# Linear attention, a top-2 mixture of experts and a squared-ReLU MLP on one core: the order of the k'v sums, where rows are normed, and the size of an untaken path

## The chip, the cores and the metric

The kernel runs on one core of one Trainium2 chip. The metric is the device time of one execution in microseconds (us). All times in this text come from the page of one profiled execution, from answers of its trace, or from the list of timed runs.

## The reference

Three layers follow each other on 2304 rows (4 batches of 576) of 512 columns (8 heads of 64):

```python
kv = np.einsum('bhsd,bhse->bhde', k, v)            # 64x64 per batch and head
out = np.einsum('bhsd,bhde->bhse', q, kv)
out = out / sqrt(mean(out * out, -1) + 1e-6) * g_norm
logits = x @ w_gate;  noisy = logits + log1p(exp(x @ w_noise)) * noise
top2, top2_w = two largest of 8 experts, softmax over the two
out[rows of e] += top2_w * (relu(x[rows of e] @ w1[e]) @ w2[e])     # 512 -> 1024 -> 512
h = relu(x @ w_in);  y = (s * h * h + b) @ w_out                     # 512 -> 2048 -> 512
```

## The kernel before

The 2304 rows are 18 tiles of 128 rows: per pair of batches eight tiles of main rows and one tile (8 and 17) of the 64 last rows of both batches.

**The front** (about the first 94 us) makes the normed attention rows. The helper `kv(b, h0, h1)` sums k'v of the heads h0 to h1 into one PSUM tile: for every head four products over 128 rows (the main rows, line 344) and then one over the 64 last rows (line 345). Even heads write partitions 0 to 63 of the tile, odd heads 64 to 127. `warm(n)` issues n products on a constant, whose result nobody reads. A batch's products are asked for in two halves or at once, between tiles, as the table KV_AT says (batch 1 after tile 1, batch 2 after tiles 5 and 6, batch 3 after tiles 10 and 11).

The loop over tiles t is written out by hand, and each engine takes its instructions in that order: transposes of q for tile t+1 (`q_tr`, line 404, evicted by ScalarE in line 406); the copy of q for tile t+3 (`repack`, on DVE up to tile 9, on POOL from tile 10, line 394); the inverse norm of tile t-1 (`inv_rms`, ScalarE lines 443 and 444, POOL lines 446 to 448); the product with k'v (`att`, line 415); its eviction (line 426), squares (430) and sums of squares (DVE, line 434) in `squares`, which also ends the inverse norm of tile t-1 (`inv_end`, DVE line 455, then POOL line 457); the logits of tile t-1 (`norm`, DVE line 465); and the store of a row tile to `xs` in DRAM (`put_rows`, SP line 470). A stored row has 520 columns: 512 unnormed ones and 8 inverse norms. From tile 9 on, the gating of the first nine tiles is spread over these steps by `tick()`: its small DVE and POOL instructions end in a list of rows `idx_e` (line 535) and two gathers from `xs` on POOL's queue (line 187). The rows are multiplied by their inverse norms after the gather (`normed`, line 211, DVE), transposed (line 378), and split into a high and a low part (lines 381 and 382). Then the experts' first product starts (lines 808 to 810). SP's queue carries loads of q, k and v, the stores to `xs`, and from tile 12 on the weights; `advance(n)` splits the weights of unit n-1 (ScalarE lines 146 and 153, DVE 148, POOL 154) and loads two units ahead.

**The main part** runs 16 groups of row blocks. Every step is a first product (`l1`), side work from a table of steps, and a second product (`l2`, lines 832 to 834). Side work brings in the next group's rows: gather, `normed`, transposes, split.

**The general path** `general()` stands after step 20. It handles inputs in which one expert gets more rows than its blocks hold. Two flags are loaded into registers, and each engine jumps over the path's two parts when they are zero, as here. The second part (from line 888) holds eight copies of `block`, one for each expert, and each copy has its eight steps over the hidden columns written out.

Of the kernel before, what the change touches and what calls it, by code (L numbers as in the profile page):

```python
# [8 lines left out]
F32 = mybir.dt.float32  # L9
# [7 lines left out]
OP = mybir.AluOpType  # L17
# [4 lines left out]
def kernel(  # L22
# [62 lines left out]


    XS = DM + H
    NROW = 8
# [119 lines left out]

    def normed(r):
        x = r[:, :DM].rearrange("p (h d) -> p h d", h=H)  # L210
        nc.vector.tensor_mul(x, x, r[:, DM:][:, :, None].to_broadcast([P, H, D]))
        return r[:, :DM]


# [53 lines left out]

    warm(12)

# [66 lines left out]
    def kv(b, h0=0, h1=H):  # L337
        K, V, KR, VR = (KQV[b, n] for n in ("k", "v", "kr", "vr"))
        ps = KVP[b] = KVP.get(b) or small_ps([P, NP, D])
        for h in range(h0, h1):  # L340
            hp, i = divmod(h, 2)
            o = ps[i * D:(i + 1) * D, hp, :]
            for j in range(NJ):
                nc.tensor.matmul(o, lhsT=K[:, h, j, :], rhs=V[:, h, j, :], start=j == 0, stop=False)
            nc.tensor.matmul(o, lhsT=KR[:, h, :], rhs=VR[:, h, :], start=False, stop=True)
        if h1 == H:
            KVP[b] = kvc = pool.tile([P, 2, 2, D], F32, name="kvc", bufs=1)
            nc.scalar.activation(kvc, ps.rearrange("p (s a) d -> p a s d", s=2), AF.Copy)
            for i in range(2):
                r = slice(i * D, (i + 1) * D)  # L350
                nc.scalar.activation(kvbd[b][r, :, i * HW_:i * HW_ + D], ps[r], AF.Copy)
# [86 lines left out]
    def inv_rms(t):  # L438
        raw, ss, x = AT[t]
        y = pool.tile([P, H], F32, name="iv", bufs=3)  # L440
        u = pool.tile([P, H], F32, name="iu", bufs=2)
# [9 lines left out]
    def inv_end(t):  # L451
        if t < 0:
            return
        raw, u, y, x = AT[t]
        nc.vector.scalar_tensor_tensor(x[:, DM:], u, 1.5, y, op0=OP.add, op1=OP.mult)
        yb = x[:, DM:].rearrange("p (a b) -> p a b", a=NP)[:, :, :, None]
        nc.gpsimd.tensor_mul(raw, raw, yb.to_broadcast([P, NP, 2, W2C]))
        AT[t] = (raw, x)

    def norm(t):  # L460
        pl, x = AT.pop(t)
        tick()
        tick()
        tick()
        nc.vector.tensor_reduce(lg[:, t, :], pl.rearrange("p a b c -> p c (a b)"), axis=AX, op=OP.add)
        XO.append((t, x))
# [72 lines left out]
    def gate_rank(g):  # L539
# [12 lines left out]
        if g == 0:  # L552
            yield from early_table(0, NT0, 0, EB, idx_e)
            for i in range(EB):
                ROWS[0, i] = gather_rows(0, i)
            yield 7
            for i in range(EB):
                ROWS[0, i] = normed(ROWS[0, i])
            yield 6
            for i in range(EB):  # L560
                put_x(0, ROWS.pop((0, i)), i)
# [152 lines left out]
    kv(0, 0, H // 2)  # L714
    warm(10)
    kv(0, H // 2, H)
    load_batch(2, "kv")
    warm(4)
    mfold_a(0)
# [15 lines left out]
    for t in range(NT + 1):  # L735
# [21 lines left out]
        if t == NT0:  # L757
            chain[:] = [gating(0), 0]
        if t == 12:
            advance(0)  # L760
        if 13 <= t < 17:
            advance(t - 12)
    put_rows()
# [20 lines left out]
    def combine(g, i, rows):  # L784
        if groups[g][0] == "e":
            return normed(rows)
        t = groups[g][2] + i
# [65 lines left out]
    def general():  # L853
# [8 lines left out]
        def block(e, icol, rows_out):  # L862
            ic = gp.tile([P, 1], I32, name="ic", bufs=1)
            nc.vector.tensor_copy(ic, icol)
            gather(rows, xs[:, :], ic)
            normed(rows)
            pt = psum.tile([P, KC, P], F32, name="ph", bufs=3)
            for c in range(KC):
                nc.tensor.transpose(pt[:, c, :], rows[:, c * P:(c + 1) * P], ident)
            nc.vector.tensor_scalar(xT, pt, gcol, None, op0=OP.mult)  # L870
            y = psum.tile([P, DM], F32, name="ph", bufs=3)
            for f in range(NF1):
                a, b = weight_aps(e * NF1 + f)
                nc.sync.dma_start(r1, a)
                nc.sync.dma_start(r2, b)
                ph = psum.tile([P, P], F32, name="ph", bufs=3)
                for c in range(KC):
                    nc.tensor.matmul(ph, lhsT=r1[:, c, :], rhs=xT[:, c, :], start=c == 0, stop=c == KC - 1)
                nc.scalar.activation(h, ph, AF.Relu)
                nc.tensor.matmul(y, lhsT=h, rhs=r2, start=f == 0, stop=f == NF1 - 1)  # L880
            yr = rows[:, :DM]
            nc.vector.tensor_copy(yr, y)
            nc.sync.dma_start(rows_out, yr)
# [4 lines left out]
        with tc.If(v1 > 0):  # L888
# [5 lines left out]
            nc.vector.tensor_scalar(idx_ov, pt, float(N // 2), None, op0=OP.add)  # L894
            for e in range(E):
                ve = nc.values_load(nblk[0:1, e:e + 1], min_val=0, max_val=NT)
                vb = nc.values_load(ovb[0:1, e:e + 1], min_val=0, max_val=OVB)
                with tc.If(ve > MB):
                    with tc.For_i(MB, ve) as blk:
                        block(e, idx_ov[:, e * NT:(e + 1) * NT][:, bass.ds(blk, 1)],  # L900
                              ys[bass.ds((vb + blk - MB) * P, P), :])

# [85 lines left out]
    at(4, rest_of_first)  # L988
    at(6, lambda: [normed(ROWS[1, i]) for i in range(groups[1][3])])
    at(5, lambda: run(gate_slots(1)))  # L990
# [11 lines left out]
    def put_first():  # L1002
        for i in range(groups[1][3]):
            put_x(1, ROWS.pop((1, i))[:, :DM], i)

# [102 lines left out]
```

## Time and profile before

| | us |
|---|---|
| timed runs | 994.40, 994.58, 996.50; median 994.58 |
| the profiled execution | 996.47 |
| its span, first to last instruction | 994.7 |
| PE busy (matmul) | 960.5, 97% of the span |
| DVE busy | 542.3, 55% |
| ScalarE busy | 398.3, 40% |
| POOL busy | 133.5, 13% |

The page gives busy time for each engine and for 40 equal slices of the span (24.9 us each), the clock that was granted to PE, and the share of time in which the 16 DMA engines moved data. Answers of the trace list instructions in order of time: the start, how long it (or a merged run of it) took, engine and line, what it writes and reads, how many, and in brackets how long the engine had been idle before it and what it had waited for. Matmuls overlap each other, so the pitch from one start to the next is shorter than one matmul. A float32 matmul of the program stands in the trace as two.

### The profile page before, as it was taken

To read this page: it belongs to the slowest core of one execution; us is meant where nothing else is said; L and a number is where in the kernel's file an instruction comes from. 1 tells how busy PE (TensorE), PEld (TensorE's weight loads), DVE (VectorE), ACT (ScalarE), POOL (GpSimd) and SP (SyncE) were. 2 spreads that over 40 slices of the span, in tenths; PEclk is the share of its full clock that TensorE was granted. 3 is DMA by queue.
4 is the path that set the end of the run, shared out by engine and by line. 5 is a ranking of instruction groups with operands and counts; after the bars stand their busy time and mean duration, and the time that the engine had idled before them with its cause. 6 is when DMAs were issued, how large, how long until landed. Compare 5 with 4: busy or idle time off the path is not lost.

```text
span 994.7 us, 13902 instructions
## 1 busy us (share of the span) xinstructions
PE 960.5 (97%) x5282; PEld 828.4 (83%) x5282; DVE 542.3 (55%) x1000; ACT 398.3 (40%) x725; POOL 133.5 (13%) x196
## 2 busy tenths in 40 slices
PE   8996998979999999999999999999999999999998
PEld 5875787979999999999999999888788878887886
DVE  1448887545686877767656465434434343443333
ACT  1666334224555555646444444323222232222222
POOL 3256325101010100000000112100110010000000
PEclk8998999989999999999999999999999999999999
DMA  9965767426457584874635532200120021001001
GB/s 264 273 196 177 216 187 234 160 78 235 135 183 267 157 273 153 279 237 150 234 104 193 189 126 79 74 1 11 32 85 1 22 65 41 1 1 43 1 1 42
DMA packets 111854, 129.30 MB, mean 130 GB/s; under 512 B 14208, under 2 KB 80768, under 8 KB 111776
## 3 DMA queue, kind: packets, MB, share of 16 engines
q1 hardware_dynamic: 104320, 108.10, 33.7%
q0 software_dynamic: 6208, 20.17, 7.0%
q8 instruction: 44, 0.72, 0.3%
q14 instruction: 34, 0.28, 0.1%
q10 hardware_dynamic: 1248, 0.03, 0.1%
HBM read 93.07 MB, written 35.20 MB: 129 GB/s over the span
## 4 chain that ended last, share of the span: by engine, by line
PE 76%; DVE 1%; ACT 1%; issue 0%; ACTq 0%
PE ph L809 13%; PE ph L810 13%; PE y L832 12%; PE ph L808 12%; PE y L834 12%; PE y L833 12%; PE sps L378 2%; DVE r L818 0%; DVE xl L382 0%; ACT hh L820 0%; ACT r L817 0%; DVE r L819 0%; DVE hl L821 0%; DVE rows L841 0%; ACT xh L381 0%
## 5 line engine op out<-in xcount | busy, mean ns | idle before, releaser
L809 PE MATMUL ph<-xl,w1h 128*128 128x320 f32 (+3 forms) x832 | 277.4, 333 | 3.1 <-DVE xl L382 3.1
L808 PE MATMUL ph<-xh,w1h 128*128 128x320 f32 (+3 forms) x832 | 276.8, 333 | 1.3 <-DVE xl L382 0.7
L810 PE MATMUL ph<-xh,w1l 128*128 128x320 f32 (+3 forms) x832 | 276.8, 333 | 0.0
L832 PE MATMUL y<-w2h,hh 128*128 128x512 f32 x608 | 244.4, 402 | 5.7 <-PEq L888 5.0
L834 PE MATMUL y<-w2h,hl 128*128 128x512 f32 x608 | 238.9, 393 | 1.2 <-DVE hl L813 1.2
L833 PE MATMUL y<-w2l,hh 128*128 128x512 f32 x608 | 238.8, 393 | 0.0
L809 PEld LDWEIGHTS ph<-xl,w1h 128*128 128x128 f32 x832 | 157.0, 189 | 18.7 <-DVE xl L382 5.1
L808 PEld LDWEIGHTS ph<-xh,w1h 128*128 128x128 f32 x832 | 157.1, 189 | 16.9 <-ACT xh L381 2.3
L810 PEld LDWEIGHTS ph<-xh,w1l 128*128 128x128 f32 x832 | 157.2, 189 | 9.8
L812 ACT ACTIVATE hh<-ph 128x320 fp32r<-128x320 f32 (+2 forms) x128 | 55.9, 438 | 228.7 <-PE ph L810 228.7
L818 DVE SCALAR_TENSOR_TENSOR r<-ph,r 128x512 f32<-128x512 f32 (+1 forms) x80 | 51.1, 638 | 175.9 <-ACT r L817 175.5
L832 PEld LDWEIGHTS y<-w2h,hh 128*128 128x128 f32 x608 | 115.3, 190 | 27.2 <-issue 5.2
L834 PEld LDWEIGHTS y<-w2h,hl 128*128 128x128 f32 x608 | 114.9, 189 | 27.3 <-DVE hl L813 1.6
L813 DVE SCALAR_TENSOR_TENSOR hl<-ph,hh 128x320 fp32r<-128x320 f32 (+2 forms) x128 | 62.3, 489 | 133.3 <-ACT hh L812 132.3
L833 PEld LDWEIGHTS y<-w2l,hh 128*128 128x128 f32 x608 | 115.3, 190 | 20.8
L817 ACT ACTIVATE r<-ph 128x512 f32<-128x512 f32 (+1 forms) x80 | 44.5, 556 | 187.9 <-PE ph L810 187.9
L820 ACT ACTIVATE hh<-r 128x512 fp32r<-128x512 f32 (+1 forms) x80 | 47.1, 589 | 101.2 <-DVE r L819 101.2
L821 DVE TENSOR_TENSOR hl<-r,hh 128x512 fp32r<-128x512 f32 (+1 forms) x80 | 51.1, 639 | 52.6 <-ACT hh L820 52.6
L187 POOL DMA_INDIRECT rows<-xs,idx x35 | 34.5, 985 | 321.7 <-PE sps L378 195.9
L187 POOL DMA_INDIRECT rows<-ys,slot_i x36 | 34.5, 958 | 268.5 <-DVE rows L790 134.3
L148 DVE SCALAR_TENSOR_TENSOR w1l<-raw,gcol,w1h 128x512 fp32r<-128x512 f32 x64 | 50.6, 792 | 15.9 <-ACT w1h L146 15.6
L153 ACT ACTIVATE w2h<-raw 128x512 fp32r<-128x512 f32 x80 | 49.6, 620 | 1.0 <-DMA raw<-in_moe_w_dram 1.0
(166 smaller groups left out, 875.9 us busy)
## 6 DMA issues: line engine op xcount, KB each, us to landing
raw<-in_moe_w_dram SPq DMA_DIRECT2D x128, 256.0 KB, 3.3
ys<-rows SPq DMA_DIRECT2D x40, 256.0 KB, 3.8
c_raw<-in_moe_w_in_dram SPq DMA_DIRECT2D x16, 512.0 KB, 6.2
c_raw<-in_moe_w_out_dram SPq DMA_DIRECT2D x16, 512.0 KB, 7.9
wd<-c_fl SPq DMA_DIRECT2D x16, 512.0 KB, 4.5
raw<-wd SPq DMA_DIRECT2D x32, 256.0 KB, 2.8
ys<-zero SPq DMA_DIRECT2D x13, 512.0 KB, 5.0
xs<-x SPq DMA_DIRECT2D x18, 260.0 KB, 3.8
```

What stands on the lines that cost most here:

```text
L148: nc.vector.scalar_tensor_tensor(l1.rearrange(fl), r1.rearrange(fl), gcol, h1.bitcast(F32).rearrange(fl), op0=OP.mult, op1=OP.subtract)
L187: nc.gpsimd.indirect_dma_start(out=dst, out_offset=None, in_=src, in_offset=bass.IndirectOffsetOnAxis(ap=icol, axis=0))
L808: nc.tensor.matmul(ps[:, :wd], lhsT=w1h[:, c, :], rhs=xh[:, c, cs], start=c == 0, stop=False)
L809: nc.tensor.matmul(ps[:, :wd], lhsT=w1h[:, c, :], rhs=xl[:, c, cs], start=False, stop=False)
L810: nc.tensor.matmul(ps[:, :wd], lhsT=w1l[:, c, :], rhs=xh[:, c, cs], start=False, stop=c == KC - 1)
L812: nc.scalar.activation(hh[:, cs], ps[:, :wd], AF.Relu)
L813: nc.vector.scalar_tensor_tensor(hl[:, cs], ps[:, :wd], 0.0, hh[:, cs].bitcast(F32), op0=OP.max, op1=OP.subtract)
L818: nc.vector.scalar_tensor_tensor(r[:, :wd], ps[:, :wd], 0.0, r[:, :wd], op0=OP.max, op1=OP.mult)
L821: nc.vector.tensor_sub(hl[:, cs], r[:, :wd], hh[:, cs].bitcast(F32))
L832: nc.tensor.matmul(y, lhsT=hh[:, cs], rhs=w2h, start=f == 0, stop=False)
L833: nc.tensor.matmul(y, lhsT=hh[:, cs], rhs=w2l, start=False, stop=False)
L834: nc.tensor.matmul(y, lhsT=hl[:, cs], rhs=w2h, start=False, stop=f == nf - 1)
```

## The change

It has these parts. `kv` runs over the row chunks on the outside and over the heads inside, so that the products over the 64 last rows stand together at the end, and products into partitions 0 to 63 and 64 to 127 alternate; one start flag per half of the partitions serves all heads. The warm-up products change from 12, 10 and 4 to 14, 4 and none. The norm is multiplied into the row tile in `norm`, before the store; a stored row has 512 columns, and `normed` and its calls are gone. Weights are loaded and split one tile earlier. The general path loops over experts and hidden columns by registers, and sums its second product in SBUF.

```diff
-    XS = DM + H
+    XS = DM
-    warm(12)
+    warm(14)
 def kv(b, h0=0, h1=H):
-        for h in range(h0, h1):
-            hp, i = divmod(h, 2)
-            o = ps[i * D:(i + 1) * D, hp, :]
-            for j in range(NJ):
-                nc.tensor.matmul(o, lhsT=K[:, h, j, :], rhs=V[:, h, j, :], start=j == 0, stop=False)
-            nc.tensor.matmul(o, lhsT=KR[:, h, :], rhs=VR[:, h, :], start=False, stop=True)
+        for j in range(NJ + 1):
+            for h in range(h0, h1):
+                hp, i = divmod(h, 2)
+                lh, rh = (K[:, h, j, :], V[:, h, j, :]) if j < NJ else (KR[:, h, :], VR[:, h, :])
+                nc.tensor.matmul(ps[i * D:(i + 1) * D, hp, :], lhsT=lh, rhs=rh, start=j == 0 and h - h0 < 2,
+                                 stop=j == NJ and h >= h1 - 2, skip_group_check=True)
 def inv_end(t):
-        nc.vector.scalar_tensor_tensor(x[:, DM:], u, 1.5, y, op0=OP.add, op1=OP.mult)
+        nc.vector.scalar_tensor_tensor(y, u, 1.5, y, op0=OP.add, op1=OP.mult)
 def norm(t):
         tick()
         tick()
         tick()
+        xv = x.rearrange("p (h d) -> p h d", h=H)
+        nc.vector.tensor_mul(xv, xv, y[:, :, None].to_broadcast([P, H, D]))
         nc.vector.tensor_reduce(lg[:, t, :], pl.rearrange("p a b c -> p c (a b)"), axis=AX, op=OP.add)
 def gate_rank(g):
-            yield 7
-            for i in range(EB):
-                ROWS[0, i] = normed(ROWS[0, i])
-            yield 6
+            yield 12
     kv(0, 0, H // 2)
-    warm(10)
+    warm(4)
     kv(0, H // 2, H)
     load_batch(2, "kv")
-    warm(4)
...
-        if t == 12:
+        if t == 11:
             advance(0)
-        if 13 <= t < 17:
-            advance(t - 12)
+        if 12 <= t < 16:
+            advance(t - 11)
 def combine(g, i, rows):
         if groups[g][0] == "e":
-            return normed(rows)
+            return rows
 def block(e, icol, rows_out):
-            normed(rows)
-            for f in range(NF1):
+            with tc.For_i(0, NF1) as f:
...
-                nc.tensor.matmul(y, lhsT=h, rhs=r2, start=f == 0, stop=f == NF1 - 1)
+                nc.tensor.matmul(y, lhsT=h, rhs=r2, start=True, stop=True)
+                nc.vector.tensor_add(yr, yr, y)
 def general():
-            for e in range(E):
+            with tc.For_i(0, E) as e:
```

Three places show how instructions move. On PE, between tile 1 and tile 2 of the front, the products of batch 1 (`kr` and `vr` are the 64 last rows); a row with x4 stands for four instructions. Before:

```order
L415 MATMUL att<-kvbd_162,qT 128x160 x4
L344 MATMUL sps<-v,k 64x64 x4
L345 MATMUL sps<-vr,kr 64x64
L344 MATMUL sps<-v,k 64x64 x4
L345 MATMUL sps<-vr,kr 64x64
L344 MATMUL sps<-v,k 64x64 x4
```

The pair of rows stands eight times there, once for each head. In the changed kernel:

```order
L410 MATMUL att<-kvbd_164,qT 128x160 x4
L339 MATMUL sps<-v,k 64x64 x32
L339 MATMUL sps<-vr,kr 64x64 x8
L399 MATMUL sps<-ident,qc 128x128 x4
L410 MATMUL att<-kvbd_164,qT 128x160 x4
```

The change from 128-row to 64-row operands is made once and no longer after every head. The second place is DVE, at tiles 12 and 13 of the front, from the tables of the gating (`ohe`) to the list of rows `idx_e`. Before:

```order
L525 TENSOR_SCALAR ohe<-io_188,early 128x256 x9
L465 TENSOR_REDUCE lg<-raw 128x16
L428 COPY raw<-att 128x128
L434 TENSOR_REDUCE ss<-sq 128x8
L455 SCALAR_TENSOR_TENSOR x<-iu,iv 128x8
L465 TENSOR_REDUCE lg<-raw 128x16
L148 SCALAR_TENSOR_TENSOR w1l_81<-raw_970,gcol,w1h_80 128x512
L428 COPY raw<-att 128x128
L535 TENSOR_SCALAR idx_e<-sps 128x2
```

In the changed kernel:

```order
L522 TENSOR_SCALAR ohe<-io_190,early 128x256 x9
L461 TENSOR_TENSOR x<-x,iv 128x512
L462 TENSOR_REDUCE lg<-raw 128x16
L147 SCALAR_TENSOR_TENSOR w1l_81<-raw_896,gcol,w1h_80 128x512
L423 COPY raw<-att 128x128
L429 TENSOR_REDUCE ss<-sq 128x8
L450 SCALAR_TENSOR_TENSOR iv<-iu,iv 128x8
L461 TENSOR_TENSOR x<-x,iv 128x512
L462 TENSOR_REDUCE lg<-raw 128x16
L147 SCALAR_TENSOR_TENSOR w1l_85<-raw_900,gcol,w1h_84 128x512
L423 COPY raw<-att 128x128
L532 TENSOR_SCALAR idx_e<-sps 128x2
```

One 128x512 multiplication (x by iv) per tile has come in, and one more weight split stands ahead of the list. The third place is PE at the general path; shown is the start of the first part's only block. Before:

```order
L885 COMPARE_AND_BRANCH
L886 COMPARE_AND_BRANCH
L886 UNCONDITIONAL_BRANCH x2
L1103 BRANCH_PREFETCH_HINT
L869 MATMUL ph<-ident,xl_2546 128x128 x4
```

After these stand eight times four products (line 878) and one (line 880), 44 products in the block, and the second part has eight such blocks and 36 products on tables. In the changed kernel the whole block is:

```order
L861 MATMUL ph<-ident,xl_2541 128x128 x4
L866 COMPARE_AND_BRANCH
L866 UNCONDITIONAL_BRANCH x2
L1095 BRANCH_PREFETCH_HINT
L872 MATMUL ph<-xh_2540 128x128 x4
L875 MATMUL ph<-gr_2542,xl_2541 128x512
L866 REGISTER_ALU
L866 COMPARE_AND_BRANCH
L866 UNCONDITIONAL_BRANCH
```

Nine products stand in a block instead of 44, and the second part has one block instead of eight beside its 36 products on tables.

## Rows read from the trace of the kernel before

**Rows 1.** The page: PE's busy tenths in 40 equal slices of the span.
```profile
PE   8996998979999999999999999999999999999998
```
**Rows 2.** By stretch: length; busy PE, PEld, DVE, ACT, POOL; PE's clock, DMA share, GB/s.
```profile
50.00:57.00 7.00, 6.09 (x60) 5.12 (x57) 2.14 (x7) 5.33 (x14) 3.42 (x7) 1.00 1.03 312
62.00:70.00 8.00, 8.00 (x87) 6.82 (x86) 5.47 (x17) 4.11 (x10) 4.58 (x13) 1.00 0.19 70
64.10:93.65 29.55, 21.23 (x189) 17.87 (x187) 21.63 (x58) 21.10 (x49) 18.78 (x36) 0.88 0.45 144
220.00:620.00 400.00, 400.00 (x2319) 364.83 (x2318) 263.29 (x409) 202.25 (x346) 37.57 (x40) 1.00 0.56 186
```
**Rows 3.** PE in order of time at k'v of batch 3 and around (start, length, idle).
```profile
53.68 1.31 PE L419 MATMUL att<-kvbd,qT 128*64 128x160 f32 x16
...
57.59 1.99 PE L415 MATMUL att<-kvbd,qT 128*128 128x160 f32 x8 [1.47 <-ACT kvbd L370]
59.37 1.06 PE L404 MATMUL sps<-ident,qc 128*128 128x128 f32 x4
...
62.07 0.68 PE L344 MATMUL sps<-v,k 128*64 128x64 f32 x8
62.68 0.32 PE L345 MATMUL sps<-vr,kr 64*64 64x64 f32 x2
62.93 0.68 PE L344 MATMUL sps<-v,k 128*64 128x64 f32 x8
...
76.29 1.25 PE L415 MATMUL att<-kvbd,qT 128*128 128x160 f32 x8
```
**Rows 4.** SP in order of time: the load of q for batch 3 is issued.
```profile
49.31 0.39 SPq L235 DMA_DIRECT2D q<-in_q_dram  x1
```
**Rows 5.** DMA issues, 40 to 70 us: count, KB, median us from issue to landing.
```profile
q<-in_q_dram SPq DMA_DIRECT2D x1, 1024.0 KB, 7.7
```
**Rows 6.** POOL, then DVE, in order of time at tile 9's inverse norm.
```profile
62.18 1.04 POOL L394 TENSOR_TENSOR qc<-q,ones 128x512 f32<-128x512 f32 x1
...
64.11 0.31 DVE L455 SCALAR_TENSOR_TENSOR x<-iu,iv 128x8 f32<-128x8 f32 x1
```
**Rows 7.** DVE groups from 64.1 to 93.65 us: count, busy us, mean ns, idle before.
```profile
L148 DVE SCALAR_TENSOR_TENSOR w1l<-raw,gcol,w1h 128x512 fp32r<-128x512 f32 x3 | 4.4, 1460 | 0.0
L465 DVE TENSOR_REDUCE lg<-raw 128x16 f32<-128x128 f32 x6 | 2.2, 366 | 3.8 <-POOL raw L457 3.8
L211 DVE TENSOR_TENSOR rows<-rows 128x512 f32<-128x512 f32 x2 | 1.5, 780 | 0.0
```
**Rows 8.** All row multiplications from 80 to 180 us: ns min, median, max.
```profile
L211 DVE TENSOR_TENSOR rows<-rows x10: 677/686/1239, 88.4 to 166.4; 128x512 f32<-128x512 f32 x10
```
**Rows 9.** PE in order of time: the front's end, the first expert group, two later waits.
```profile
82.71 1.35 PE L415 MATMUL att<-kvbd,qT 128*128 128x160 f32 x8 [1.94 <-ACT qT L406]
89.09 1.97 PE L378 MATMUL sps<-ident,rows 128*128 128x128 f32 x8 [5.03 <-DVE rows L211]
...
93.65 0.39 PE L808 MATMUL ph<-xh,w1h 128*128 128x256 f32 x1 [0.74 <-DVE xl L382]
...
163.85 0.93 PE L378 MATMUL sps<-ident,rows 128*128 128x128 f32 x5 [1.27 <-DVE hl L813]
...
173.63 0.41 PE L809 MATMUL ph<-xl,w1h 128*128 128x320 f32 x1 [1.88 <-DVE xl L382]
```
**Rows 10.** PE's sequencer at the general path's two jumps: ns, start.
```profile
L885 PEldq COMPARE_BRANCH  x1: 353/353/353, 208.1 to 208.1; - x1
L888 PEldq COMPARE_BRANCH  x1: 4501/4501/4501, 209.9 to 209.9; - x1
```
**Rows 11.** PE in order of time behind the second jump.
```profile
214.70 0.77 PE L832 MATMUL y<-w2h,hh 128*128 128x512 f32 x1 [5.01 <-PEq L888]
...
218.64 0.39 PE L832 MATMUL y<-w2h,hh 128*128 128x512 f32 x1
218.88 0.40 PE L833 MATMUL y<-w2l,hh 128*128 128x512 f32 x1
```

## What the change was predicted to do

> **What bounds the kernel now.** The first view to read is the page's picture of busy tenths [rows 1]: PE's digits are uneven over the first nine slices, and 9 in nearly every one behind them. The windows confirm it: from 220 to 620 us PE was busy 400.00 of 400.00 us at a granted clock of 1.00, with DVE at 263.29 and ScalarE at 202.25 [rows 2]. So the end is the moment at which that dense stretch starts, plus PE work that the change does not touch. Only what PE loses ahead of about 220 us can be won or made worse: idle time, stretches at the lower clock, and products that take longer than they must. Three places there are touched: the front up to the first expert product at 93.65 us, two waits in the next expert groups [rows 9], and the general path's second jump [rows 10, 11]. The sum is made against the profiled execution (996.47 us); the median of the timed runs, 994.58, lies 1.89 below it, and this is taken off at the end.
>
> **k'v's order.** Before, the next head's products start .86 us behind a head's (62.07 to 62.93) [rows 3]: eight over 128 rows and two over 64 (each float32 product stands twice), so a half call of four heads takes 3.46 us. The eight take .68, and one alone lasts about .22 (an estimate: the .32 of two over 64 rows less a start-to-start of .10), so their pitch is (.68 - .22) / 7 = .065; the last of the eight then starts at 62.53 and the first over 64 rows at 62.68, so a change between 128 and 64 rows costs about .15 in place of a pitch, twice per head. After, a half call has 40 products and one such change: 39 x .065 + .15 = 2.7 us, .75 saved. More is possible where products into the two halves of the partitions run beside each other. The row that shows it is the product with k'v on tile 8, that of the last rows: 16 half-height matmuls in 1.31 us, where eight full ones took 1.25 [rows 3]. With that a half call takes about 1.5 us, 2 saved. Four half calls (batches 1 and 2) stand ahead of batch 3's: 3 to 8 us, if PE is what the front waits for.
>
> **What binds behind it.** It is not PE alone. The load of q for batch 3 was issued at 49.31 and took 7.7 us [rows 4, 5]; it lands at 57.0, with all 16 DMA engines in use from 50 to 57 us (share 1.03) [rows 2], so it comes no earlier. POOL's copy of tile 13 reads that q and stands ahead of tile 9's inverse norm in POOL's queue: it started at 62.18, took 1.04, and DVE ended the inverse norm at 64.11, 1.93 behind its start [rows 6]. With the data at 57.0 that step cannot come before 57.0 + 1.93 = 58.9. This caps PE's gain at 64.11 - 58.9 = 5.2 us, in the middle of the 3 to 8. From here on the front is a race of PE with DVE. In the 29.55 us to the first expert product DVE was busy 21.63 [rows 2]. The change adds six multiplications of 128x512 (one per tile in `norm`, six being the count of L465 there) at .69, the median of the ten [rows 7, 8]: +4.1. It removes the two of `normed`: 2 x .78 = -1.6 [rows 7]. It moves one more weight split ahead of the list `idx_e`: +1.46 [rows 7], or half if it is not slowed. DVE's work becomes 24.9 to 25.6. Of DVE's 7.9 idle us the largest part, 3.8, waits for POOL's product of the logits [rows 7]; the multiplication now lies exactly in that wait, so I keep a third of the idle time, 2.4, as what the added work cannot fill. 58.9 + 25.6 + 2.4 = 86.9, and the first expert product comes at about 87.0 instead of 93.65: **-6.6 us**, with -4 (all idle time stays and splits are slow) to -9 (DVE idles nowhere) as ends.
>
> **What goes with the multiplication.** The 5.03 us for which PE waited on the gathered rows [rows 9] end in DVE's multiplication by the list of waits, but most of it is the gather's own time: behind the gather the rows were multiplied for 2 x .78 us. After, the transposes wait for the gather directly. Since `put_rows` on SP now follows the multiplication, a store starts .69 later than the inverse norm would allow; behind it in SP's queue stand the loads of the weights, at a DMA share of .19 from 62 to 70 us [rows 2], so there is room. The list `idx_e` and the gathers come after all nine early stores in any case. Eight columns fewer in a stored row change nothing that a row here shows.
>
> **Warm-ups.** Two products more at the start, six and four fewer behind k'v's first half and the second. Nearest row of the same width: .24 per product [rows 11], .43 at half clock, so -8 net is 2 to 3.5 us of PE. It is costed at nothing, since the tiles there wait for loads up to the q that lands at 57.0; if that cover were gone it would be a gain of that size. It can also hurt, which is a rival below.
>
> **Expert groups 1 and 2.** The change takes the multiplication out of DVE's queue in the main part, where it stands in front of the evictions that PE waits for. At 163.85 PE waited 1.27 us for hl, at 173.63 1.88 for xl [rows 9], both DVE's. Without 2 x .69 ahead the first goes nearly to zero (-1.1), the second loses .69: **-1.8 us**, between 0 (the rows' arrival is what binds) and -3. Behind 220 us PE has no idle time [rows 2], so some thirty multiplications less on DVE are worth nothing there.
>
> **The general path.** The jump over the first part, one block of 44 products, held PE's sequencer .35 us; the jump over the second, eight such blocks and 36 products on tables, held it 4.50 us [rows 10], and PE was idle 5.01 [rows 11]. Then nine products started .43 us apart (214.70 to 218.64, half clock) instead of .24: 3.94 - 9 x .24 = 1.8 more. After, the second part has 36 products and one block of 9, as long as what the jump of .35 passed. That row is the near one, so I take .3 of stall and no loss of clock: 5.01 - .3 + 1.8 = **-6.5 us**, with 0 as the other end. The Trainium skill ("Runtime: NRT & Kernel Launch", Instruction fetch mechanics) states that a taken branch out of the instructions already fetched waits for a fetch by DMA. The two rows agree in kind, and the same sentence speaks of loops by registers as costly; none of these runs here, so its price would be paid only by the one jump.
>
> **Sum.** 996.47 - 6.6 - 1.8 - 6.5 = 981.57 for a profiled run, less 1.89: **979.7 us**.
>
> **Rivals.** (a) The second jump stalls as before, because what counts is not the length passed but that the target has to be fetched at all. For it: 36 products on tables remain. Against it: the .35 row. No -6.5: 986.2 us. (b) The front gains 1 us instead of 6.6. PE that finishes k'v sooner waits longer for loads, and fewer warm-ups fill that wait; the product and transposes at 57.59 behind an idle 1.47 took 1.99 + 1.06 at half clock, where the same product later took 1.25 [rows 3]. Some seven tiles at 1.99 - 1.25 = .74 more eat 5 of the gain, or DVE's added work does. It gives 985.3 us. The Trainium skill ("TensorE: Matmul & The Clock Gate", Loop structure matters more than you think) warns of just this: matmuls with waits for DMA between them run cold. The 1.99 agrees; by that rule alone the front's part would be near zero and the result that of this rival. (c) Slower: DVE is the front's bound from its first tile, and each of 18 multiplications stands on the path, 18 x .69 - 1.6 = +10.8. With -6.5 and -1.8 that is +2.5: 997.1 us. It decides where DVE has no idle time left; against it, DVE was busy 2.14 of 7.00 us from 50 to 57 [rows 2]. (d) Better: halves run beside each other everywhere, q is copied as soon as it lands, and with waits shorter than about 1.3 us PE keeps its clock: -9.5 in the front, -3 in the groups and -7.5 at the jump: 974.6 us.
>
> **How the numbers follow.** The forecast has .52, (a) .15, (b) .15, (d) .10, (c) .08. The forecast's own ends, with one term off at a time, run from 976 to 983; the range reaches to (a) and (b) above and (d) below: 974 to 987. It leaves out (c) and the outer halves of the others, about .18. About 0.2%, 2 us, is what a measurement of this kernel can tell from no change. Only (c) can lie there or above: .03 within, .05 slower; the other .92 is faster.
>
> **What the changed profile would show.** At the second jump: a sequencer row near .35 instead of 4.50 and full pitch behind it; with a row of 4 us, (a) holds. In the front: k'v's 40 products of a half call in under 2.7 us; POOL's copy of tile 13 near 57; the first expert product near 87; PE's transposes behind the gather waiting for a DMA and not for DVE. If PE's pitch of .43 and clock below 1.00 fill more of the front, (b) holds; if DVE is busy without a break up to the list, (c) does. In the groups: the waits of 1.27 and 1.88 shorter. I would be wrong in kind if the dense stretch at 220 us started earlier by 15 us and the end did not follow, which would mean that something behind it waits for other than PE.

## The result and the profile after

The changed kernel took 983.37 us (median of four runs, 982.76 to 986.96) against 995.54 for the kernel before (four runs, 994.40 to 999.86): a ratio of .9877, interval .9838 to .9916. A second set of five runs gave 983.98 and .9881 (.9863 to .9900). Forecast were 979.7 us and a gain of 14.9 us; the gain is 12.2 in the first set and 10.9 in the second. The profiled execution after has a span of 982.0 us, 12.7 less than before. Sign and range held; two of the three terms of the sum came out smaller than said and one larger, for reasons that the forecast did not have.

The page after: PE's busy tenths and its clock in 40 slices, which answer to [rows 1].

```profile
PE   7866999999999999999999999999999999999998
...
PEclk7987999999999999999999999999999999999999
```

The later slices that read 8 and 7 before are 9 now; the first three are lower than before (786 against 899). PE has less to do there and waits more: 4.0 us in sum for loads of v, and once 5.5 us for DVE. Windows of the changed kernel follow (length; busy PE, PEld, DVE, ACT, POOL; granted clock, DMA share, GB/s), as in [rows 2]:

```profile
59.09:87.83 28.74, 16.61 (x114) 14.62 (x112) 24.55 (x60) 17.19 (x39) 19.94 (x36) 0.73 0.50 163
...
79.00:92.50 13.50, 9.29 (x45) 7.66 (x45) 10.61 (x27) 7.53 (x18) 9.28 (x18) 0.50 0.69 223
106.30:109.70 3.40, 3.40 (x14) 3.03 (x13) 3.40 (x10) 0.00 (x0) 1.32 (x1) 0.50 0.80 232
...
220.00:620.00 400.00, 399.24 (x2312) 363.56 (x2311) 250.42 (x390) 201.94 (x348) 39.76 (x41) 1.00 0.55 184
```

From 220 us on PE is as dense as before (399.24 of 400). DVE has 13 us less work there (250.42 against 263.29 in [rows 2]), and nothing comes of it. So the end still follows the start of the dense stretch.

PE of the changed kernel in order of time (start, length, engine and line, tiles, count, in brackets the idle time before and what it waited for), against [rows 3, 9]:

```profile
52.47 1.15 PE L339 MATMUL sps<-v,k 128*64 128x64 f32 x32
53.55 0.45 PE L339 MATMUL sps<-vr,kr 64*64 64x64 f32 x8
53.93 0.66 PE L399 MATMUL sps<-ident,qc 128*128 128x128 f32 x4
...
66.12 0.50 PE L542 MATMUL sps<-g,onesb 128*128 128x72 bf16 x9 [5.50 <-DVE g L510]
...
83.60 1.97 PE L373 MATMUL sps<-ident,rows 128*128 128x128 f32 x8 [3.63 <-DMA rows<-xs,idx_e]
85.50 2.40 PE L414 MATMUL att<-kvbd,qT 128*64 128x160 f32 x16
87.83 0.58 PE L801 MATMUL ph<-xh,w1h 128*128 128x256 f32 x1
...
92.36 0.41 PE L802 MATMUL ph<-xl,w1h 128*128 128x256 f32 x1
92.57 0.32 PE L803 MATMUL ph<-xh,w1l 128*128 128x256 f32 x1
```

A half call of k'v takes 53.93 - 52.47 = 1.46 us instead of 3.46. PE's lead then turns into a wait of 5.50 us for the gating on DVE. The transposes behind the gather wait for the DMA and no longer for DVE, and the first expert product stands at 87.83. From 79.0 to 92.5 us the clock is .50 of full speed (1.2 of 2.4 GHz), so the expert products start .21 us apart (92.36 to 92.57) until then.

The steps that the forecast took as binding in the front are on SP, POOL and DVE. SP's row comes first (the load of q for batch 3 is issued), then the DMA, POOL (the copy of tile 13), and DVE (the inverse norm of tile 9, then the list of rows):

```profile
47.78 0.41 SPq L229 DMA_DIRECT2D q<-in_q_dram  x1
```

```profile
q<-in_q_dram SPq DMA_DIRECT2D x1, 1024.0 KB, 9.3
```

```profile
57.17 1.04 POOL L389 TENSOR_TENSOR qc<-q,ones 128x512 f32<-128x512 f32 x1 [2.56 <-PE sps L339]
```

```profile
59.09 0.28 DVE L450 SCALAR_TENSOR_TENSOR iv<-iu,iv 128x8 f32<-128x8 f32 x1 [3.28 <-POOL iu L443]
...
77.26 0.14 DVE L532 TENSOR_SCALAR idx_e<-sps 128x2 int32<-128x2 f32 x1
```

The q lands at 47.78 + 9.3 = 57.1, and POOL starts .1 us behind it. The bracket on POOL's row names PE; a wait for several events is put down to one of them, and the landing time tells which it was (in the second profile of this kernel, further down, the copy again starts .1 us behind the landing, and the row names the load). DVE's groups from 59.09 to 87.83 us (count, busy us, mean ns, idle before), as in [rows 7]:

```profile
L147 DVE SCALAR_TENSOR_TENSOR w1l<-raw,gcol,w1h 128x512 fp32r<-128x512 f32 x4 | 5.1, 1276 | 0.0
L461 DVE TENSOR_TENSOR x<-x,iv 128x512 f32<-128x512 f32 x6 | 4.1, 686 | 0.1
...
L462 DVE TENSOR_REDUCE lg<-raw 128x16 f32<-128x128 f32 x6 | 2.2, 364 | 3.3 <-POOL raw L452 3.3
```

And the general path: the sequencer's jump, PE on both sides of it, and DVE, as in [rows 10, 11]:

```profile
L882 PEldq COMPARE_BRANCH  x1: 339/339/339, 202.3 to 202.3; - x1
L882 DVEq COMPARE_BRANCH  x1: 56/56/56, 204.5 to 204.5; - x1
L882 DVEq EVENT_SEMAPHORE  x2: 21/21/21, 207.3 to 207.4; - x2
```

```profile
202.93 0.47 PE L825 MATMUL y<-w2h,hh 128*128 128x512 f32 x1 [0.84 <-PEq L882]
...
207.42 0.39 PE L801 MATMUL ph<-xh,w1h 128*128 128x320 f32 x1 [0.84 <-DVEq L882]
```

```profile
207.56 0.75 DVE L147 SCALAR_TENSOR_TENSOR w1l<-raw,gcol,w1h 128x512 fp32r<-128x512 f32 x1 [4.12 <-DVEq L882]
```

**Where the time went.** Both kernels issue the same 4,320 products of the experts and the last layer, so the nth of one can be laid against the nth of the other; the difference of their starts is what the change has won up to there.

| product | before, us | after, us | difference |
|---|---|---|---|
| first expert product | 93.65 | 87.83 | -5.8 |
| first product of the second kind (`y`) | 97.45 | 93.44 | -4.0 |
| the 91st | 112.17 | 109.26 | -2.9 |
| last before the general path | 208.95 | 201.33 | -7.6 |
| behind it, past DVE's jump | 220.03 | 207.42 | -12.6 |
| the last of all | 989.64 | 976.76 | -12.9 |

So 2.9 us of the front's 5.8 arrive at 112 us, the expert groups up to the general path add 4.7, the general path 5.0, and the rest of the span .3.

### The profile page after: what moved, and what is told of

The parts are those of the page before. It is cut to its first block, busy times and chain, and to the rows that moved or that the text cites. A ratio compares the mean times of both kernels' runs of the same rounds, so it can differ in the third digit from the quotient of the medians.

```text
span 982.0 us, 13843 instructions
## 1 busy us (share of the span) xinstructions
PE 942.6 (96%) x5274; PEld 818.5 (83%) x5275; DVE 529.9 (54%) x979; ACT 397.8 (41%) x726; POOL 140.3 (14%) x197
## 4 chain that ended last, share of the span: by engine, by line
PE 77%; DVE 1%; ACT 1%; issue 0%; ACTq 0%
PE ph L802 13%; PE ph L803 13%; PE ph L801 13%; PE y L825 12%; PE y L826 12%; PE y L827 12%; PE sps L373 2%; DVE r L811 0%; DVE xl L377 0%; ACT hh L813 0%; ACT r L810 0%; DVE r L812 0%; DVE hl L814 0%; DVE rows L834 0%; ACT xh L376 0%
## 5 line engine op out<-in xcount | busy, mean ns | idle before, releaser
L801 PEld LDWEIGHTS ph<-xh,w1h 128*128 128x128 f32 x832 | 158.0, 190 | 17.6 <-ACT xh L376 2.3
L805 ACT ACTIVATE hh<-ph 128x320 fp32r<-128x320 f32 (+2 forms) x128 | 55.9, 437 | 227.0 <-PE ph L803 227.0
L147 DVE SCALAR_TENSOR_TENSOR w1l<-raw,gcol,w1h 128x512 fp32r<-128x512 f32 x64 | 50.7, 793 | 22.3 <-ACT w1h L145 17.6
```

What stands on the lines that cost most here:

```text
L147: nc.vector.scalar_tensor_tensor(l1.rearrange(fl), r1.rearrange(fl), gcol, h1.bitcast(F32).rearrange(fl), op0=OP.mult, op1=OP.subtract)
L801: nc.tensor.matmul(ps[:, :wd], lhsT=w1h[:, c, :], rhs=xh[:, c, cs], start=c == 0, stop=False)
L805: nc.scalar.activation(hh[:, cs], ps[:, :wd], AF.Relu)
```

## The experiments

Medians stand beside the median of the kernel before that was timed along with them. Single runs of the changed kernels spread by some 4 us, so a difference under 2 us is read from the traces or not at all.

**The general path put back.** The edit restores the eight written-out copies of the block:

```diff
-            with tc.For_i(0, E) as e:
+            for e in range(E):
...
-            with tc.For_i(0, NF1) as f:
+            for f in range(NF1):
```

> The changed kernel with the general path as before (eight copies of the block, 44 products each). Theory A, from the two traces laid against each other product by product: the smaller path gives 5.2 us (6.0 on PE, of which .84 is given back in a new wait for DVE behind the jump), so +5.2: 988.6 us, and PE is idle 5 us at the second jump again. Theory B, the forecast's own sum: 6.5, 989.9 us. Theory C: the gain lies elsewhere and a later wait takes it, 983.4 us.

988.57 us (before 995.06; ratio .9940, .9920 to .9959), 5.2 more than the changed kernel's first set of runs and 4.6 more than its second: theory A, while B's 6.5 is not excluded by the intervals. The profiled execution was the slowest of the seven (993.94; its q of batch 3 landed at 59.4), so only the stretch in question is read from it:

```profile
L880 PEldq COMPARE_BRANCH  x1: 3681/3681/3681, 208.0 to 208.0; - x1
```

```profile
211.97 0.77 PE L825 MATMUL y<-w2h,hh 128*128 128x512 f32 x1 [4.19 <-PEq L880]
```

```profile
210.20:217.00 6.80, 5.03 (x12) 3.99 (x13) 1.35 (x2) 1.25 (x2) 0.00 (x0) 0.50 0.32 105
```

The jump stalls again (3.68 us), PE is idle 4.19, and the products behind it run at a granted clock of .50 until 217.0 us. Between the last product ahead of the general path and the one past DVE's jump this kernel gains .3 us on the kernel before, where the changed one gains 5.0.

**The k'v order put back.**

```diff
-        for j in range(NJ + 1):
-            for h in range(h0, h1):
+        for h in range(h0, h1):
+            for j in range(NJ):
```

> The changed kernel with k'v summed head by head as before. Theory A: PE is what the front waits for until the q of batch 3 has landed; POOL's copy of tile 13 starts near 62 instead of 57.2 and the first expert product comes 5 us later, near 93, of which about 3 us reach the end, since a stretch of half clock then lies over other work: 986.4 us. Theory B: loads and DVE bind, PE's order is worth under 1 us: 984 us or less.

991.42 us (before 995.06; .9960, .9946 to .9974): 7.4 to 8.1 more than the changed kernel, above both theories. In its trace the q of batch 3 lands at 55.9, but POOL's copy starts only at 61.35, without an idle time ahead of it, and the first expert product stands at 92.0:

```profile
61.35 1.04 POOL L388 TENSOR_TENSOR qc<-q,ones 128x512 f32<-128x512 f32 x1
```

So it is not the load that the copy follows here, nor PE directly: POOL comes to it from the steps of the tiles before, and these run late. At 52.91 us DVE had waited 2.62 for ScalarE's eviction of a PE product. That is theory A's start near 62, reached by way of DVE and POOL. The profiled execution was the lowest of ten runs (988.30), and its last product comes 4.5 us later than in the changed kernel. What the other runs lost beyond that no trace shows.

**The k'v order alone**, in the kernel before (the same edit the other way round).

> The kernel before with nothing changed but the order of the k'v sums. Theory A: PE was what the front waited for, so POOL's copy of tile 13 starts as soon as its q lands, near 57 instead of 62.2, the multiplication is not yet in DVE's way, and the first expert product comes 5 to 6 us earlier than in the kernel before; with most of it kept to the end: 989.5 to 991 us. Theory B: the order pays only together with the fewer warm-up products, since 14 of them stand in PE's queue ahead of batch 0's second half and behind it; then 992 to 994 us.

989.15 us (before 994.90; .9935, .9918 to .9952): theory A, 5.75 us from this edit with every warm-up product in place. POOL in order of time, then DVE at tile 9's inverse norm:

```profile
59.70 1.04 POOL L395 TENSOR_TENSOR qc<-q,ones 128x512 f32<-128x512 f32 x1 [3.35 <-DMA q<-in_q_dram]
61.62 0.28 DVE L456 SCALAR_TENSOR_TENSOR x<-iu,iv 128x8 f32<-128x8 f32 x1 [3.32 <-POOL iu L449]
```

Now the load is what ends POOL's wait, here at 59.7, since in this run it landed late; the first expert product stands at 88.08 nevertheless. The inverse norm comes only 2.5 us earlier than in the kernel before (61.62 for 64.11), the product 5.6. The rest is won between the inverse norm and the list, which takes 14.5 us (61.62 to 76.14) instead of 17.6 (64.11 to 81.72). DVE's copy out of the product with k'v in that stretch, in the kernel before and here:

```profile
L428 DVE COPY raw<-att 128x128 f32<-128x128 f32 x4 | 1.1, 284 | 2.9 <-ACT x L426 2.9
L429 DVE COPY raw<-att 128x128 f32<-128x128 f32 x4 | 1.1, 275 | 0.0
```

Batch 3's own half calls stood there on PE [rows 3], and DVE waited 2.9 us in all for ScalarE's eviction of products that came late.

**No alternation of the halves.** All even heads, then all odd heads:

```diff
-        for j in range(NJ + 1):
-            for h in range(h0, h1):
+        for j, h in [(j, h) for i in range(2) for j in range(NJ + 1) for h in range(h0 + i, h1, 2)]:
```

> The changed kernel with the k'v products of all even heads first (into partitions 0 to 63) and then those of all odd heads; the last rows still stand at the end of each of the two runs. Theory A: products into the two halves run beside each other only because they alternate, so without that a half call (1.46 us from 52.47 to 53.93 in the changed kernel) takes 40 products at the pitch of the kernel before, .058 to .065, and three changes of height: 2.6 to 3.0 us. PE has then 1.2 us less of its lead per half call, and the front loses up to 3 us: 984 to 987 us. Theory B: the gain is the fewer changes between 128 and 64 rows alone, and a half call stays near 1.5 to 1.8 us: 983.5 us.

986.64 us (before 996.16; .9910, .9888 to .9931), theory A by its median, though the interval still touches that of the changed kernel; what decides is the trace. PE of that kernel in order of time:

```profile
57.64 1.15 PE L338 MATMUL sps<-v,k 128*64 128x64 f32 x16
58.71 0.44 PE L338 MATMUL sps<-vr,kr 64*64 64x64 f32 x4
59.08 1.15 PE L338 MATMUL sps<-v,k 128*64 128x64 f32 x16
60.16 0.44 PE L338 MATMUL sps<-vr,kr 64*64 64x64 f32 x4
60.53 0.66 PE L398 MATMUL sps<-ident,qc 128*128 128x128 f32 x4
```

16 products take the 1.15 us in which the changed kernel does 32, and a half call takes 60.53 - 57.64 = 2.89 us instead of 1.46. Products into the two halves of the partitions run side by side when they alternate; the fewer changes of height alone give .57 of the 2.0 us. The Trainium skill ("TensorE: Matmul & The Clock Gate", Why this matters for your kernels) says that small outputs placed in different groups of partitions run concurrently; the two kernels agree, with a factor of 2.0.

**The norm behind the gather again**, with rows of 520 columns.

```diff
-        nc.vector.tensor_mul(xv, xv, y[:, :, None].to_broadcast([P, H, D]))
...
+            for i in range(EB):
+                ROWS[0, i] = normed(ROWS[0, i])
```

> The changed kernel with the norm multiplied in behind the gather as before (rows of 520 columns). Theory A: the added multiplications stand in DVE's queue ahead of the list of rows, four of .69 us, so the list comes 2.7 us earlier without them and the two behind the gather cost 1.5: the first expert product near 86.6 instead of 87.8; in the expert groups the 4.5 us that the trace shows as won come back for the most part, so +2 to +4: 985.4 to 987.4 us. Theory B: the multiplication's place is worth the forecast's 1.8 us in the groups and costs as much in the front: 983.4 us.

982.56 us (before 995.06; .9880, .9855 to .9904), the same as the changed kernel: theory B. The first expert product stood at 86.06, 1.8 and .7 earlier than in the two profiles of the changed kernel, and in the groups its PE waits for DVE's multiplication again:

```profile
114.89 1.33 PE L378 MATMUL sps<-ident,rows 128*128 128x128 f32 x8 [0.73 <-DVE rows L211]
```

Two later waits for DVE were longer than in the changed kernel (.80 instead of .30 for hl, and 1.87 instead of 1.48 for xl). The changed kernel's PE never waits for such a multiplication there, and pays for it in the front and right behind it.

**The k'v order and the general path alone**, nothing else of the change.

> The kernel before with the new order of the k'v sums and the looped general path, and nothing else of the change. Theory A: the two parts bring 5.8 and 5.2 us apart, and they add up, since they lie at different ends of the first 220 us: 983.9 us, and moving the norm, the warm-ups and the weights is worth nothing that can be told from no change. Theory B: the other parts are worth the forecast's 1.8 us in the expert groups and more in the front: 986 us or more here.

982.45 us (before 996.16; .9860, .9838 to .9881). Theory A holds: the two parts make the whole gain, and the moved norm, the warm-ups and the earlier weights together are worth nothing that these runs tell from zero (the intervals leave some 3 us). None of the three was run alone in the kernel before.

**Weights one tile later.**

```diff
-        if t == 11:
+        if t == 12:
```

> The changed kernel with the weights loaded and split one tile later, as before. Theory A: one split of 1.45 us fewer stands ahead of the list on DVE, so list and first expert product come 1 to 1.5 us earlier: 982 to 982.5 us. Theory B: the first weights are then what the first product waits for, 1 to 2 us later: 984.5 to 985.5 us.

985.01 us (before 995.06; .9911, .9882 to .9939; the four runs lie at 983.1 to 983.4 and 986.6 to 987.3). Inconclusive by time. The trace bears out the first half of theory A: with one split fewer ahead of it the list comes 16.5 us behind tile 9's inverse norm (57.37 to 73.87), where the changed kernel's two profiles have 18.2 and 18.0. What becomes of these 1.5 us is not shown. Behind the first product (83.83) PE waits 1.18 us for xl and 2.08 for hl, the changed kernel .58 and 1.04 in one profile and 1.77 and none in the other; neither these nor theory B's wait for the weights can be told from the difference between two runs.

**PE kept busy over the gather.**

```diff
             yield 12
+            warm(12)
...
+        if t == 16:
+            warm(9)
```

> The changed kernel with products on a constant in two places where PE waits at the end of the front: 9 ahead of tile 16's product (2.57 us idle before) and 12 ahead of the transposes of the gathered rows (3.63 us idle). Theory A: the clock stays up behind the gather, so the transposes take 1.0 instead of 1.97 us, tile 17's product 1.3 instead of 2.4, and the first 24 expert products (.21 us apart up to 92.6) run at .12: 3.5 to 4.2 us less, 979 to 980.5 us. Theory B: the clock falls a little later instead, as it did at 106.3 us for 3.4 us, and gives half of that back: 981.5 us. Theory C: PE's clock there is hidden by DVE and the weights: 983.4 us.

982.72 us (before 994.90; .9878, .9860 to .9897), 1.3 below the changed kernel timed along with it, whose interval contains it: theory C is nearest, A is refuted, and B's 981.5 is not excluded. The clock did stay up where it was meant to:

```profile
82.84 1.04 PE L373 MATMUL sps<-ident,rows 128*128 128x128 f32 x8
83.81 1.31 PE L414 MATMUL att<-kvbd,qT 128*64 128x160 f32 x16
87.38 0.35 PE L804 MATMUL ph<-xh,w1h 128*128 128x256 f32 x1 [2.27 <-DVE xl L377]
```

1.04 and 1.31 instead of 1.97 and 2.40: 2.0 us faster on PE, all of it waited away for DVE's `xl` (2.27 us), which stands behind DVE's work for tiles 15 and 16 and two weight splits. The clock fell all the same, at 87.7, .3 us behind the first product and its wait, and stayed at .50 until 91.1 us.

**Multiplications of tiles 9 to 13 deferred** past the list.

```diff
+        XD.append((t, x, y))
+        for _ in range(0 if NT0 <= t < 14 else 1 if t < NT0 else 2 if t < 17 else len(XD)):
```

> The changed kernel with the multiplications of tiles 9 to 13 left for steps 14 to 17, behind the list of rows in DVE's queue; nothing is left out. Theory A: four of .69 us leave the chain to the list, which comes 2.5 us earlier as in the kernel that multiplies behind the gather, while the expert groups keep what they won: the first expert product near 85.5 us, and 980 to 981.5 us in all. Theory B: the end of the front then has DVE as its bound, five more multiplications stand before the low parts of the split rows, and what was won at the list is given back: 983 to 984 us.

986.72 us (before 994.90; .9908, .9889 to .9925): theory B, and worse than that. The list came 17.8 us behind POOL's copy (58.0 to 75.8) instead of 20.1, but then, in PE's and DVE's order of time:

```profile
96.73 0.79 PE L831 MATMUL y<-w2h,hl 128*128 128x512 f32 x1 [3.61 <-DVE hl L810]
```

```profile
94.31 2.03 DVE L465 TENSOR_TENSOR x<-x,iv 128x512 f32<-128x512 f32 x3
96.26 0.74 DVE L810 SCALAR_TENSOR_TENSOR hl<-ph,hh 128x256 fp32r<-128x256 f32 x2
```

The last three multiplications stand in front of the `hl` for which PE waits 3.61 us.

**POOL's order.** The inverse norm of tile t-1 ahead of the copy of q:

```diff
+        if t >= 10:
+            inv_rms(t - 1)
         if t + 3 < NT:
             repack(t + 3)
```

> The changed kernel with the inverse norm of tile t-1 ahead of the copy of q for tile t+3 in POOL's queue, from step 10 on. Theory A: POOL then does not stand behind the q of batch 3 when tile 9's inverse norm is due; ScalarE's part of that was done at 56.6 us in the changed kernel, so DVE ends the inverse norm near 57.3 instead of 59.1 and the chain to the list and the first expert product come 1.5 to 1.8 us earlier: 982 to 982.5 us. Theory B: DVE has no idle time up to the list and the later copies come later, nothing moves: 983.5 to 984 us.

983.29 us (before 996.16; .9866, .9845 to .9888). DVE ended tile 9's inverse norm at 57.95 + .75 = 58.7, where it had been 59.4, and the list came at 75.81 instead of 77.26 (77.12 in the second profile of the changed kernel). The first expert product stood at 86.93, between the two profiles of the changed kernel (87.83 and 86.71); at the 91st product it is level with the second profile of the changed kernel, both 4.4 us ahead of the kernel before. Theory B for the time, A only for the list. DVE in order of time:

```profile
57.95 0.75 DVE L450 SCALAR_TENSOR_TENSOR iv<-iu,iv 128x8 f32<-128x8 f32 x1
```

> The same order on POOL in the kernel that multiplies the norm in behind the gather. Theory A: that kernel's first expert product stood at 86.06 us; it comes 1.5 us earlier, and the end with it: 981 to 981.5 us. Theory B: nothing moves: 982.5 us.

981.60 us (before 996.16; .9850, .9828 to .9871; five runs from 978.70 to 982.19): nearest to theory A, and B's 982.5 lies within the interval. The first expert product stood at 85.14, .9 earlier than without that order; that is one profile of each, and the two profiles of the changed kernel differ by more. This is the lowest median of all kernels, 14.6 below its kernel before; its interval overlaps that of the changed kernel, so it is not shown to be better.

**The changed kernel once more.**

> The changed kernel itself once more, beside the others of this call. In the traces so far the moment at which the q of batch 3 lands differs between runs (55.3 to 59.4 us), and where k'v is summed in the new order POOL's copy follows it at once. Theory A: so the front follows the loads and the times spread over some 4 us, 983 to 987, with a median near 984. Theory B: the first runs spread by chance of this one chip only, and the times agree within 1.5 us.

983.98 us (before 994.90), runs from 982.01 to 984.60: between the theories. Its q landed at 57.1 and the copy started at 57.19:

```profile
57.19 1.04 POOL L389 TENSOR_TENSOR qc<-q,ones 128x512 f32<-128x512 f32 x1 [0.32 <-DMA q<-in_q_dram]
```

In all eight kernels that sum k'v in the new order and leave POOL's order as it was, the copy starts within .5 us of the landing, which lies between 55.3 (weights one tile later) and 59.4 us (general path put back).

## Why the prediction was right, and where its terms were off

**k'v's order** went as its upper case said: 2.0 us saved per half call, by products side by side. The forecast had left open whether they overlap; the kernel without alternation settles it. **The cap by the load** came out at its step: forecast q at 57.0 and the inverse norm at 58.9, measured 57.1 and 59.09. That they agree so closely is in part luck, since the same load landed anywhere from 55.3 to 59.4 us in the profiles. And it caps the step, not the front. With the k'v order alone the step came 2.5 us earlier and the first expert product 5.6, the median 5.75, above the cap of 5.2: the forecast counted the half calls ahead of batch 3's and gave no price to batch 3's own, behind the step, which had held DVE up by 2.9 us. In the changed kernel DVE's added work took that place.

**DVE behind it.** The six multiplications cost 4.1 us as said (L461 x6), and the one split more cost .7, the lower of the two counts. DVE was busy 24.55 us against 24.9 to 25.6, and idle 28.74 - 24.55 = 4.2 against 2.4: POOL's product of the logits still held it for 3.3 us, because the gathers stand on POOL in between and one multiplication of .69 cannot fill that. Product at 87.83 instead of 86.9, -5.8 instead of -6.6; 86.71 in the second profiled run.

**What happened behind the first product** is the step that failed. The forecast counted the front's gain at the first expert product and took it as banked. Before, the half clock behind the gather ended at 92.3 us and the experts began at 93.65 at full clock; after, they began 5.8 us earlier, inside the half clock that lasted to 92.6, and a second stretch from 106.3 to 109.7 took another part: -5.8 became -2.9. By the kernel that fills the gather with products the clock is not the only bound there, since DVE's `xl` is as late.

The record shows more on this than the clock. In the four profiles of kernels that multiply behind the gather the lead over the kernel before is nearly kept from the first product to the 91st: 5.6 and 5.6 us (k'v order alone), 7.2 and 5.9 (with the general path), 7.6 and 8.3 (norm behind the gather), 8.5 and 8.3 (the same with POOL's new order). In all nine profiles with the multiplication ahead of the store it shrinks, by 1.8 to 8.3 us. The kernel with the k'v order put back does so without the clock: from its first product to the 91st the clock was 1.00, and it still lost 1.8 us, with waits of 1.11 us for `xl`, .31 for `hh` and 2.09 for `hl`, where the kernel before has .69 for `hh` and 1.18 for `hl`:

```profile
92.00:112.37 20.37, 16.53 (x130) 14.07 (x129) 18.30 (x57) 8.07 (x19) 8.14 (x14) 1.00 0.45 141
```

In the changed kernel three of the multiplications stand on DVE between `xl` and the first `hl`; the last of them:

```profile
93.37 0.69 DVE L461 TENSOR_TENSOR x<-x,iv 128x512 f32<-128x512 f32 x1
...
94.64 0.75 DVE L806 SCALAR_TENSOR_TENSOR hl<-ph,hh 128x256 fp32r<-128x256 f32 x2
```

So an early first product can be banked where DVE keeps up behind it. The forecast put DVE's added work into the way to the first product and counted none of it behind.

**The expert groups** brought 4.7 instead of 1.8. The two waits of the forecast fell from 1.27 to .30 and from 1.88 to 1.48, 1.4 us in sum, and all of PE's waits over .15 us there from 5.4 to 3.7. The other 3.0 go with two stretches of half clock that the kernel before had and the changed one has not. Windows of before:

```profile
136.80:139.80 3.00, 3.00 (x8) 2.39 (x8) 2.93 (x8) 0.00 (x0) 0.00 (x0) 0.50 0.37 113
174.20:177.60 3.40, 3.40 (x15) 3.40 (x14) 1.52 (x4) 0.44 (x1) 2.75 (x3) 0.50 0.93 279
```

In the changed kernel the clock is 1.00 over the whole of it, and past the general path too:

```profile
109.80:219.00 109.20, 103.81 (x619) 91.93 (x618) 64.35 (x171) 39.28 (x75) 28.21 (x25) 1.00 0.61 192
```

Half of such a stretch is lost, 1.7 us of each (the first lasts from 136.7 to 140.1). Whether it occurs is not this change's doing: the second profile of the same changed kernel had one from 132.5 to 135.9 and none at 106, and there the groups brought 3.0. So front and groups gave 7.6 us in sum where 8.4 was forecast, but that is luck as far as the clock made it: what the front lost behind the first product the groups brought back, and the forecast had neither.

**The general path** gave 5.0 in the traces and 4.6 to 5.2 in the medians instead of 6.5. The jump itself went as said: .34 us instead of 4.50, and full pitch behind it. Two terms were missed. PE was idle .84, not .3, since around the branch its sequencer has other steps on semaphores. And DVE's own jump, hidden before under PE's, came to light: the branch at 204.5 took .06, the next step of DVE's sequencer came at 207.3, DVE was idle 4.12, and PE waited .84 for it. That these 2.7 us belong to the jump is read from their place (the same gap was 3.5 us before, over the longer code); the trace has no name for them. The forecast priced the jump on PE only.

Rival (a) is refuted by the .34 us, (c) by the gain. Rival (b) was half right: the front's gain did shrink by the clock and by DVE, though to 2.9 and not to 1, and behind the first product instead of ahead of it. Of (d) the first two conditions came true, and the third did not: the clock fell at 106.3 us with no wait ahead of it. Nor does the forecast's split by cause hold: the kernel with two of the parts alone is as fast as the whole. The move of the norm, which the forecast credited with 1.8 in the groups, brought about 1 there (the two waits are .30 and 1.45 to 1.48 us in the nine profiles that have it, .73 to 1.13 and 1.86 to 1.89 in the four that have not), and took at least as much at and behind the first product. The warm-ups, costed at nothing, have no run of their own, so their price stays open within the 3 us above.

## What to carry to other kernels

Follow a gain past the point where it is first seen: what was early at the first expert product ran into the wait for the next engine wherever that engine had been given more work, or into a clock that had not yet come back. Small products into different halves of the partitions should alternate; ordered one half after the other, the same work took twice as long. A branch over code that never runs is not free: each engine pays by itself, and the price went down with the length of that code (4.50 to .34 us on PE, but only 3.5 to 2.7 on DVE), so the next engine's stall shows once the first one's is gone.

## What the runs showed of the hardware

The granted clock also fell while PE was never idle. In the changed kernel PE was busy 3.40 of 3.40 us from 106.3 to 109.7 at a clock of .50, and ahead of it stood 27 products of one column each:

```profile
103.58 2.30 PE L528 MATMUL sps<-ncen_h,ohe 128*128 128x1 f16 x27
```

In the kernel before, 12 products of 40 columns, behind a wait of .74 us, stood ahead of the stretch from 136.7 to 140.1. But the changed kernel has the same 12 products at 130.38 without such a stretch in one profile, and with one in the other; what decides between them these runs don't show.

Once PE was out of the way, the front followed the loads, and what a load takes differs between runs: the q of batch 3 landed between 55.3 and 59.4 us in eleven profiles of kernels with the new order, and two of these kernels that differ from the changed one only behind that load had it at 55.8 and 59.4 (its own two profiles at 57.0 and 57.1). That moves POOL's copy, and tile 9's inverse norm behind it, by as much. How much of the spread of 4 to 5 us between runs it makes is open: the kernel before, whose front waited for PE, spreads as much (994.40 to 999.86).
